# A short convolution in 8 steps of 16 channels, half-row matmuls in pairs, and a new written order, in a two-layer SSM and MLP kernel

## The chip, the cores and the metric

The kernel runs on one core of one Trainium2 chip. The metric is the device time of one execution in microseconds (us). The kernel before takes 224.44 us, the median of three runs (224.42 to 224.55). A profile of one execution gives the time of every instruction on every engine. PE is the matrix engine (TensorE), PEld its weight loads, DVE is VectorE, ACT is ScalarE, POOL is GpSimd, and SP issues most of the DMAs.

## The reference, cut to what matters

```python
B, S, D = 1, 2048, 640; ks = 4; F = 1728            # bf16 tensors
def _A_ref(q, k, v, shift_k, ssm_k, ssm_D):          # q is the layer-normed x
    k_shift[s, d] = sum over t in 0..3 of k[s - 3 + t, d] * shift_k[d, ks - 1 - t]
    kv = k_shift * v
    y = causal convolution of kv with ssm_k along s (by FFT of length 2 S)
    y = y + kv * ssm_D
    return q * y
def _B_ref(x, w1, b1, w2):
    h = x @ w1 + b1                                  # 640 -> 1728
    return (h * tanh(softplus(h))) @ w2              # Mish, 1728 -> 640
x = A_q
h = x + _A_ref(layernorm(x), A_k, A_v, A_shift_k, A_ssm_k, A_ssm_D)
out = h + _B_ref(layernorm(h), B_w1, B_b1, B_w2)
```

Only the convolution along the sequence, the skip term `kv * ssm_D` and the two matmuls of the MLP matter for what follows.

## The kernel before, in words

The 2048 positions are seen as 128 partitions by 16 (`NT`) positions each. The 640 channels are five blocks of 128, and these are grouped into three chunks: blocks 0 and 1, blocks 2 and 3, and block 4.

The first half of the kernel does the long convolution by transforms written as matmuls. Every matmul result lands in one of eight PSUM banks and has to be copied out (evicted) by ACT or DVE before the bank can be used again. The steps, with the names that the written order uses:

- `k1pe`/`k1ev` (L625): the filter `ssm_k`, loaded as `rn`, is transposed on PE, eight 128x128 transposes for each half of a block, and evicted.
- `dadd` (L620): the skip term. `ssm_D` is loaded as one row and added to the first row of the transposed filter, which is position 0 of the filter, by one small instruction for each block on POOL (four) and DVE (one).
- `s1kpe`/`s1kev` (L543, L544): first transform of the filter. Two matmuls with 64 weight columns each write the two halves of a bank, and run side by side in the array.
- `ktpe`/`ktev` (L571), `ktsh` (L585): the key `A_k` is transposed into `kt_s` and a copy shifted by one partition is made on POOL.
- `wsh` (L501), `coef` (L493), `cfpe` (L487): the weights of the short convolution. One matmul spreads `shift_k` over 128 partitions, four DVE copies lay it into `coef` with zeros around it, and four POOL multiplications by a mask make banded weights.
- `kspe` (L595, L596) and `kv` (L600): the short convolution. A step takes 4 positions by 32 channels as its 128 rows. Each step needs one matmul with 128 output columns for its own positions and one with 96 columns for the carry from the step before. DVE multiplies each result with the value and so makes `kv`.
- `s2kpe`/`s2kev` (L652): second transform of the filter with the table `G`. `sw` (L668, L669) are DMAs that exchange neighbouring partitions of the result, in two pieces for each chunk.
- `s1v`, `s2v` (L685): the same two transforms for `kv`. `p2` (L710) and `p1` (L706) are the products with the filter, elementwise in bf16. For chunk 0 there are four pieces of 128x2048, and each piece has one `p2` and one `p1`: six of these eight run on DVE, two on POOL.
- `i1pe`/`i1ev` (L743, L744): first inverse transform. It needs all products of its chunk.

The second half is the MLP. `i2p` (L803) and `y` are the second inverse transform for each of 16 tiles of 128 positions. `lnx`, `wb`, `h`, `bn`, `pow`, `hc` are the elementwise parts and the second layer norm. The normalised tile `hc` is transposed: tiles 0 to 3 on PE with an eviction (`trpe` L850, `trev`), tiles 4 to 15 by a transposing DMA (`trd`, L839). The tiles form five units of 256, 256, 512, 512 and 512 columns. `m1pe` (L898) multiplies a unit with `w1`, `hb` (L903) applies Mish, `m2pe` (L915) multiplies with `w2`, and `res` (L921) adds the residual. 1728 is 13 blocks of 128 rows and one of 64. The 64 rows go through `m1pex` (L878) for two units, or two halves of one unit, at once; their results stand in the lower and the upper 64 partitions of `hbx`. In the second matmul they are contracted over all 128 partitions by L916, the last of 14 matmuls of each result: the weights `w2[:, 13]` and `w2h` hold the 64 rows in one half and zeros (`w2z`, `w2hz`) in the other.

`fz` (L468) and `wm` (L464) are matmuls on zeros that fill waits of PE.

The order of all instructions is a list of words, `ORDER`, written out by hand or by a search outside of the kernel. Each word names a step and its engine (t PE, a ACT, v DVE, p POOL, d a DMA on SP's queue, s one on ACT's). `_schedule` walks over it, gives PSUM banks out and estimates start times, and the steps are emitted by these. Every engine does its own steps in this order, and SP its DMAs.

Of the kernel before, what the change touches and what calls it, by code (L numbers as in the profile page):

```python
# [17 lines left out]
D = 640  # L18
# [8 lines left out]
d_id:s d_sk:s wz:v d_dr:s cz:v d_go:d d_n2:d wm:t fz0:t d_n0:d k1pe2x:t warm:a k1ev2x:a d_n3:d k1pe2y:t d_n1:d cfpe:t d_n4:d k1pe0y:t k1ev0y:a  # L27
k1pe0x:t k1ev2y:v dadd2:v s1kpe2_0x:t k1ev0x:v kz:p coef:v s1kpe2_2x:t s1kpe2_1x:t s1kpe2_1y:t s1kev2_1x:v s1kev2_0x:v s1kev2_1y:v s1kpe2_3y:t
s1kev2_3y:a k1pe3x:t k1ev3x:a s1kev2_2x:a k1pe1x:t k1ev1x:v k1pe1y:t w2hz:p dadd0:p wsh0:p dadd1:p k1pe3y:t dadd3:p k1pe4y:t k1ev1y:v k1pe4x:t
k1ev3y:v k1ev4x:v dadd4:p s1kpe1_2y:t k1ev4y:a s1kpe1_3x:t s1kpe1_0x:t s1kev1_0x:v s1kpe1_0y:t s1kpe1_1x:t s1kev1_1x:v s1kpe0_1x:t s1kpe1_3y:t  # L30
s1kpe4_0y:t s1kev1_2y:a s1kpe2_2y:t s1kev1_3x:a d_k3:d d_k2:d d_x0:d s1kev0_1x:a s1kev1_0y:v s1kev1_3y:a s1kev2_2y:a s1kpe3_0x:t s1kpe0_2y:t
s1kev0_2y:a s1kpe0_1y:t s1kev3_0x:a s1kpe2_3x:t s1kev2_3x:a ktpe3y:t s1kpe0_2x:t s1kpe4_2x:t s1kev4_2x:a s1kev4_0y:v ln1_2:v s1kev0_1y:v ln1_1:v
s1kpe4_1x:t s1kpe0_0x:t s1kev4_1x:a s1kpe4_2y:t s1kpe1_2x:t s1kev0_0x:v s1kpe0_0y:t d_k1:d d_g4:d s1kev1_2x:a d_k0:d d_g5:d s1kpe3_2x:t ktpe0y:t
s1kev0_2x:a ktpe1y:t d_v1:d ktev0y:v ktpe4y:t ktev3y:v s1kpe4_0x:t ktev1y:v ktev4y:v s1kev4_2y:a s1kev0_0y:a s1kev3_2x:a s1kpe3_1y:t s1kev4_0x:a
s1kev3_1y:a s1kpe3_3x:t s1kpe3_0y:t s1kpe4_1y:t s1kev3_3x:a s1kpe0_3y:t s1kpe4_3y:t s1kpe2_0y:t s1kpe4_3x:t s1kev0_3y:v s1kev2_0y:v s1kev4_1y:a
ln1_3:v s1kev3_0y:a s1kev4_3x:a wsh1:p s1kpe3_2y:t ln1p1:p s1kpe3_1x:t s1kpe1_1y:t ktsh1:p wsh3:p s1kpe0_3x:t s1kpe3_3y:t s1kev3_1x:a ktpe2y:t
s1kev0_3x:a s1kev4_3y:a s1kev3_2y:v s1kev1_1y:v ktpe4x:t ktpe3x:t ktev3x:v ktpe1x:t s1kev3_3y:a ktev1x:v ln1_0:v ktpe0x:t s2kpe_14y:t d_g6:d d_g0:d
# [137 lines left out]
def _schedule(ops):  # L175
# [7 lines left out]
    for word in ORDER:  # L183
# [6 lines left out]
        for rt in o.allocs:  # L190
            t, rt.slot = rt.ring.free()
            est = max(est, t)
# [23 lines left out]
        for rt in o.allocs:  # L216
            rt.ring.take(rt.slot, rt)
# [9 lines left out]
def _dve1(n):  # L227
    return 0.06 + 0.001045 * n
# [740 lines left out]
```

## Time and profile before

| | |
|---|---|
| median of three runs | 224.44 us |
| profiled execution, its own time | 224.86 us |
| span in its trace | 223.1 us |
| busy PE / DVE / ACT / POOL | 214.7 / 146.2 / 134.4 / 65.7 us |
| matmuls | 2598 |

The span is what the trace covers; the 1.76 us between it and the execution's own time lie around it. "Busy" of PE counts a matmul from its start to its modelled end, and matmuls overlap, so the start times of neighbouring matmuls tell how fast PE really runs.

### The profile page before, as it was taken

How to read it: one execution, taken by the hardware profiler on the slowest of the kernel's cores; microseconds unless marked ns; L12 is line 12 of the kernel's file. 1: busy time of each engine (PE TensorE's matmuls, PEld its weight loads, DVE VectorE, ACT ScalarE, POOL GpSimd, SP SyncE). 2: the span in 40 equal slices, each digit the busy share in tenths (PEclk: the TensorE clock that was granted, in tenths of full speed). 3: DMA queues.
4: the chain of work that ended last, by engine and by line, in shares of the span. 5: the costliest groups of instructions: out<-in, count | busy, mean ns of one | idle time of the engine just before them, and what ended most of it. 6: DMA issues, size and time to landing. Idle time of an engine off the chain costs nothing.

```text
span 223.1 us, 6218 instructions
## 1 busy us (share of the span) xinstructions
PE 214.7 (96%) x2598; PEld 162.1 (73%) x2598; DVE 146.2 (66%) x317; ACT 134.4 (60%) x268; POOL 65.7 (29%) x106
## 2 busy tenths in 40 slices
PE   7998899999999999999999999999999999999994
PEld 2988899999877999988887644576645445675773
DVE  0699989999999998999788898974400000004023
ACT  2689989999999999888870446800053454330000
POOL 1271950005596007235767714320000000000000
PEclk9999999999999999999999999999999999999999
DMA  6999991075999999100001401043350000000024
GB/s 214 388 408 424 408 413 69 3 203 193 277 290 283 319 351 347 62 3 0 3 0 32 88 0 31 0 91 60 88 179 0 1 0 3 0 0 0 32 82 153
DMA packets 27342, 30.68 MB, mean 138 GB/s; under 512 B 9393, under 2 KB 23730, under 8 KB 26930
## 3 DMA queue, kind: packets, MB, share of 16 engines
q1 hardware_dynamic: 26880, 30.10, 41.1%
q8 instruction: 20, 0.33, 0.6%
q10 hardware_dynamic: 338, 0.18, 0.3%
q14 instruction: 8, 0.07, 0.1%
q0 software_dynamic: 96, 0.00, 0.0%
HBM read 20.45 MB, written 2.62 MB: 103 GB/s over the span
## 4 chain that ended last, share of the span: by engine, by line
PE 64%; DVE 13%; DMA 7%; ACT 7%; POOL 5%; issue 2%; SPq 0%; DVEq 0%; ACTq 0%; POOLq 0%
PE ps L915 21%; PE ps L898 19%; ACT uv L419 6%; DMA x<-in_A_q_dram 5%; PE ps L743 4%; PE ps L744 4%; PE ps L652 3%; PE ps L543 2%; PE ps L571 2%; DMA rn<-in_A_ssm_k_dram 2%; DVE st L776 2%; DVE st L822 2%; PE ps L595 2%; POOL r L782 2%; PE ps L916 2%
## 5 line engine op out<-in xcount | busy, mean ns | idle before, releaser
L915 PE MATMUL ps<-rn,uv 128*128 128x320 bf16 (+2 forms) x416 | 61.1, 299 | 0.2 <-DVE x L921 0.2
L903 ACT ACTIVATE uv<-ps,b1s 128x512 bf16<-128x512 f32 (+1 forms) x65 | 35.4, 610 | 39.1 <-PE ps L898 38.5
L898 PE MATMUL ps<-G 128*128 128x512 bf16 (+1 forms) x325 | 58.6, 337 | 0.0
L915 PEld LDWEIGHTS <-uv 128*128 128x128 bf16 x416 | 40.2, 98 | 17.5 <-issue 0.4
L419 ACT CAST uk<-ps 128x512 bf16<-128x512 f32 (+1 forms) x96 | 48.7, 702 | 2.6 <-PE ps L544 1.6
L898 PEld LDWEIGHTS <-G 128*128 128x128 bf16 x325 | 31.2, 98 | 23.9 <-issue 1.1
L921 DVE TENSOR_TENSOR xb<-ps,xb 128x320 bf16<-128x320 f32 (+2 forms) x12 | 5.7, 487 | 36.3 <-PE ps L916 35.8
L419 ACT CAST uv<-ps 128x512 bf16<-128x512 f32 (+2 forms) x57 | 28.7, 845 | 0.0
L921 DVE TENSOR_TENSOR xa<-ps,xa 128x320 bf16<-128x320 f32 x12 | 5.9, 488 | 21.6 <-PE ps L916 21.6
L827 POOL TENSOR_TENSOR r<-ve,mhalf 128x1 f32<-128x1 f32 x16 | 10.0, 630 | 32.7 <-DVE ve L824 32.7
L743 PE MATMUL ps<-a,uv 128*128 128x128 bf16 x160 | 18.8, 219 | 0.2
L421 DVE CAST uk<-ps 128x512 bf16<-128x512 f32 (+1 forms) x27 | 17.2, 669 | 1.4 <-PE ps L744 0.9
L743 PEld LDWEIGHTS <-uv 128*128 128x128 bf16 x160 | 17.9, 113 | 0.0
L421 DVE CAST uv<-ps 128x512 bf16<-128x512 f32 (+1 forms) x25 | 15.3, 677 | 0.0
L685 PE MATMUL ps<-uv,G 128*128 128x64 bf16 (+1 forms) x256 | 12.8, 197 | 0.8
L685 PEld LDWEIGHTS <-G 128*128 128x128 bf16 x256 | 11.1, 96 | 3.1 <-issue 2.1
L600 DVE TENSOR_TENSOR ra<-ps,rb 128x512 bf16<-128x512 f32 x20 | 12.5, 684 | 0.3 <-PE ps L596 0.3
L419 ACT CAST rb<-ps 128x512 bf16<-128x512 f32 (+1 forms) x28 | 10.6, 495 | 2.7 <-PE ps L803 2.7
L652 PE MATMUL ps<-uk,G 128*128 128x160 bf16 x128 | 12.1, 230 | 0.0
L782 POOL TENSOR_TENSOR r<-ve,mhalf 128x1 f32<-128x1 f32 x16 | 10.8, 672 | 1.3
L706 DVE TENSOR_TENSOR uv<-uv,uk 128x2048 bf16<-128x2048 bf16 (+1 forms) x11 | 10.9, 1022 | 0.0
L544 PE MATMUL ps<-cst,ra 128*64 128x128 bf16 x160 | 10.6, 220 | 0.1
(116 smaller groups left out, 376.7 us busy)
## 6 DMA issues: line engine op xcount, KB each, us to landing
G<-tab_g SPq DMA_DIRECT2D x8, 512.0 KB, 12.9
rn<-in_A_ssm_k_dram SPq DMA_DIRECT2D x5, 512.0 KB, 6.2
ra<-in_A_k_dram SPq DMA_DIRECT2D x4, 640.0 KB, 9.9
rb<-in_A_v_dram SPq DMA_DIRECT2D x2, 1280.0 KB, 13.1
G<-in_B_w_dram SPq DMA_DIRECT2D x5, 432.0 KB, 6.4
rn<-in_B_w_dram SPq DMA_DIRECT2D x1, 2080.0 KB, 9.8
rn<-uk SPq DMA_DIRECT2D x4, 512.0 KB, 5.1
rb<-uk SPq DMA_DIRECT2D x8, 256.0 KB, 7.9
```

The source lines that it names most:

```text
L419: nc.scalar.copy(o, i)
L421: nc.vector.tensor_copy(o, i)
L600: nc.vector.tensor_tensor(kv_w[:, m, :, 8 * h:8 * h + 8, l0:l0 + n], ps.rearrange("p (l t d) -> p d t l", l=n, t=8), raw_v[:, 8 * h:8 * h ...
L652: nc.tensor.matmul(ps[:, o:o + 160], g_v[:, f, :], KA[:, :, f, :], start=True, stop=True)
L685: nc.tensor.matmul(ps[:, fl * n:fl * n + n], g_v[:, f0 + h * kf + fl, :], VX[x][:, :, f0 + h * kf + fl, :], start=True, stop=True)
L706: eng.tensor_tensor(v, v, K[c.i][:, :, f0:f1, :], ALU.mult)
L743: nc.tensor.matmul(pz[:, k, :], V[c.i][:, dg // 4, :, dg % 4], a12[:, 0, :], start=True, stop=False)
L782: nc.gpsimd.tensor_tensor(r1[:, t2:t2 + 1], ve1[:, t2:t2 + 1], mhalf[:, 0:1], ALU.pow)
L898: nc.tensor.matmul(ph[:, 0:w], w1[:, dc, fc * P:fc * P + P], lnhT_of(u)[:, dc, 0:w], start=(dc == 0), stop=(dc == NDC - 1))
L903: nc.scalar.activation(hb_of(u)[:, fc, 0:w], rt.tile[:, 0:w], ACT.Mish, bias=b1s[:, fc:fc + 1], scale=1.0)
L915: nc.tensor.matmul(po[:, 0:d1 - d0], hb_of(u)[:, fc, tl * P:(tl + 1) * P], w2[:, fc, d0:d1], start=(fc == 0), stop=False)
L921: nc.vector.tensor_tensor(x, rt.tile[:, 0:d1 - d0], x, ALU.add)
```

## The change

The change has these parts.

- The short convolution takes 8 positions by 16 channels as its 128 rows. The carry needs 48 columns in place of 96. The counts stay: 80 matmuls of each kind, 20 multiplications on DVE. `kt_s` has three slots of eight groups (before five slots of four); `ktsh` copies twice as many elements. `wsh` is ten POOL multiplications of 128x704 in place of four of 128x1120, and stands in the free part of each `kt_s` block and in `xb`. `cfpe` lays the coefficients out with their zeros by nine matmuls, and `coef` is one copy of 128x440 on ACT.
- The skip term: `ssm_D` is loaded as 32 rows of 20, four small matmuls (`dcpe`) turn it into a column for each block, one DVE copy evicts it, and `dq` adds the column to the untransposed filter, one instruction of 128x1 on DVE for each block, before the half of the transposes that reads it.
- Tiles 2 and 3 (unit 1) are transposed by DMA: 14 transposing DMAs in place of 12, two `trpe` and two `trev` fewer.
- Row pairs: the 64 remaining rows are contracted first. `m2q` takes two tiles, one with its 64 rows in the lower partitions, one in the upper, and starts their results by matmuls that use 64 rows of the array each; it takes four PSUM banks. There are eight `m2q`. The zero halves and `w2z`, `w2hz` are gone. `m1pex` lays two units out so that the pair of a tile lies in the other half.
- The products of chunk 0 are eight pieces of 128x1024, eight of the sixteen on POOL and eight on DVE; the exchange of chunk 0 is four DMAs (`sw0_0` to `sw0_3`).
- Fillers: `wm` has eight matmuls in place of nine, each of the four `fz` has two in place of one, and no `fz` stands at the front.
- `ORDER` is new throughout, with other delays in the estimates (`d_k`, `d_n`, `sw0`, `d_t2m`, `d_w1`, the fetch of instructions). The filter begins with block 0 in place of block 2. The value's half `d_v1` is issued behind four of the eight pieces of `G`, before behind two. The table `t2m` is issued after the exchanges of chunks 1 and 2 and two pieces of `w1`, before between the exchanges of chunk 1 and chunk 2. On PE the words change between steps with the array in halves (`s1`, `m1pex`, `m2q`) and all others 54 times, before 28: 32 times up to the first `i1pe` (before 22) and 22 times after it (before 6).

```diff
@@ the skip term
-        def dadd(e, kd=kd, rd=rd):
-            k = kd[0:1, 0]
-            (nc.vector if e == "dve" else nc.gpsimd).tensor_tensor(k, k, rd, ALU.add)
+        def dadd(e, n=n, b=b):
+            nc.vector.tensor_tensor(n[:, 0:1], n[:, 0:1], d_col[:, b:b + 1], ALU.add)
+        k1 = OP(f"dq{b}", ("dve", 0.1), [d_n[b], d_rows], emit=dadd)
+    def emit_dc(e):
+        for a in range(4):
+            nc.tensor.matmul(ps_f32(dc_rt)[:, 0:NDC], cst[0:32, 4 * P + 3 - a:5 * P + 3 - a], d_row[:, a:20:4], start=(a == 0), stop=(a == 3))
@@ the weights of the short convolution
     def emit_cfpe(e):
-        nc.tensor.matmul(ps_f32(cf_rt)[:, 0:80], rep4, sk_r[:], start=True, stop=True)
+        ps = ps_f32(cf_rt)[:, 0:440]
+        for i, (a, j0, j1) in enumerate(((0, 0, 4), (4, 0, 4), (7, 1, 4), (7, 0, 1), (1, 0, 4), (2, 0, 4), (3, 0, 4), (5, 0, 4), (6, 0, 4))):
+            nc.tensor.matmul(ps.rearrange("p (r t) -> p r t", t=11)[:, :, a + j0:a + j1], cst[0:16, 3 * P - 16 * a:4 * P - 16 * a],
+                             sk_r[:].rearrange("p (r j) -> p r j", j=4)[:, :, j0:j1], start=(i == 0), stop=(i == 8))
     def emit_coef(e):
-        for a in range(4):
-            ps = slice(a * 32, a * 32 + 32)
-            nc.vector.tensor_copy(coef[ps, :, a:a + 4], cf_rt.tile[ps, 0:80].rearrange("p (g j) -> p g j", j=4))
+        ev(e, coef[:], cf_rt.tile[:, 0:440])
@@ the short convolution
-                for l in (2 * k, 2 * k + 1):
-                    r = 4 * m + l
-                    for a in (2 * h, 2 * h + 1):
-                        o = ps[:, (l - 2 * k) * 256 + (a - 2 * h) * P:][:, 0:P]
-                        nc.tensor.matmul(o, t[:, l, a, :], wsh[r // 5][:, r % 5, 0:128], start=True, stop=False)
-                        nc.tensor.matmul(o[:, 0:96], t[:, l, a - 1 if a else 4, :], wsh[r // 5][:, r % 5, 128:224], start=False, stop=True)
+                for l in range(4):
+                    o, q, w = ps[:, P * l:P * l + P], 4 * k + l, wsh[m][k][:, l, :]
+                    nc.tensor.matmul(o, t[:, q, h, :], w[:, 0:128], start=True, stop=False)
+                    nc.tensor.matmul(o[:, 0:48], t[:, q, 0 if h else 2, :], w[:, 128:176], start=False, stop=True)
@@ the products of chunk 0, the transposes
-        npf = (32, 32, 32)[len(c.dcs) - 1]
+        npf = (16, 32, 32)[c.i]
-        if U_OF[t2] >= 2:
+        if U_OF[t2] >= 1:
@@ the row pairs
+            def pq(e, ab=ab, parts=parts):
+                for i in range(2):
+                    for t2 in ab:
+                        _, c, h = last64[t2]
+                        d0, d1, rt = parts[t2][i]
+                        rhs = w2h[64:P, d0:d1] if h else w2[0:64, 13, d0:d1]
+                        nc.tensor.matmul(ps_f32(rt)[:, 0:d1 - d0], hbx[64 * h:64 * h + 64, c:c + P], rhs, start=True, stop=False)
                     for fc in range(NFC - 1):
-                        nc.tensor.matmul(po[:, 0:d1 - d0], hb_of(u)[:, fc, tl * P:(tl + 1) * P], w2[:, fc, d0:d1], start=(fc == 0), stop=False)
-                    nc.tensor.matmul(po[:, 0:d1 - d0], lhs, w2h[:, d0:d1] if h else w2[:, 13, d0:d1], start=False, stop=True)
+                        nc.tensor.matmul(po[:, 0:d1 - d0], hb_of(u)[:, fc, tl * P:(tl + 1) * P], w2[:, fc, d0:d1], start=False, stop=(fc == NFC - 2))
@@ the fillers
-        for _ in range(9):
+        for _ in range(8):
```

331 lines of the change are left out of this document (171 added, 160 removed).

## The prediction

> **What bounds the kernel now.** I read the page's busy shares and slices first, then the busy time by stage, then single stretches. From the page:
>
> ```profile
> span 223.1 us, 6218 instructions
> ...
> PE 214.7 (96%) x2598; PEld 162.1 (73%) x2598; DVE 146.2 (66%) x317; ACT 134.4 (60%) x268; POOL 65.7 (29%) x106
> ...
> PE   7998899999999999999999999999999999999994
> ...
> DVE  0699989999999998999788898974400000004023
> ACT  2689989999999999888870446800053454330000
> ```
>
> PE is busy nearly everywhere, but so are DVE and ACT in the first 40% of the slices. The view of busy time by stretches separates them (columns: length, then PE, PEld, DVE, ACT, POOL busy with instruction counts, clock, DMA share, GB/s):
>
> ```profile
> 5.70:28.00 22.30, 20.39 (x472) 19.32 (x473) 19.72 (x41) 19.05 (x33) 12.58 (x14) 1.00 1.02 407
> 28.00:72.00 44.00, 42.46 (x905) 39.33 (x904) 43.08 (x67) 43.19 (x93) 18.11 (x16) 1.00 0.69 215
> 72.00:124.00 52.00, 51.81 (x623) 45.83 (x621) 47.23 (x115) 40.68 (x94) 23.50 (x46) 1.00 0.38 124
> 124.00:220.00 96.00, 95.87 (x595) 56.30 (x594) 35.36 (x94) 30.00 (x49) 10.48 (x21) 1.00 0.16 41
> ```
>
> I read two regimes. From 28 to 72 us (conv, second transforms, products) both evicting engines are full, 43.1 and 43.2 of 44 us: this stretch lasts as long as DVE and ACT together have work, and a matmul removed there frees time on an engine that waits for banks anyway. From 5.7 to 28 us DMA is full (407 GB/s, share 1.02), and DVE and ACT have gaps of 2.6 and 3.25 us. From 72 us on PE is without gaps (0.2 and 0.1 us idle), so there each matmul taken away shortens the kernel by its pitch. The granted clock is 1.00 in all of it.
>
> **The late part, 72 to 220 us.** Three things change: the 64-row contraction, its mode switches, and two transposed tiles. The chain of work shows what one matmul costs in the stream, as pieces with start and length:
>
> ```profile
> 126.06 0.14 PE ps L916
> ...
> 168.88 14.03 PE ps L898 x65
> 182.91 1.20 PE ps L878 x10
> ```
>
> 65 matmuls of 512 columns take 14.03 us, 0.216 each. One L916 of 320 columns is 0.14 (0.135 by the same rate). There are 32 of L916: 30 of 320 columns, one of 512, one of 128, together 30 x 0.135 + 0.216 + 0.054 = 4.3 us. The change issues as many, but two at a time on separate halves of the rows. If two run in the time of one, 2.15 us go. The trace of before has no halves by rows; its nearest is L878, halves by columns: ten matmuls of 512 columns in 1.20 us, which is five times 0.216 and 0.12 over. So halves by columns do overlap fully. For halves by rows the ends are 0 and -2.15; I take -2.15, by L878. The Trainium skill (TensorE: Matmul & The Clock Gate, Part 3) states that matmuls on different row strips run concurrently, which no run here shows; by it the value is the same.
>
> What speaks against it is the change of mode. In the timeline around the same L878:
>
> ```profile
> 181.67 1.24 PE L898 MATMUL ps<-G 128*128 128x512 bf16 x5
> 182.84 1.27 PE L878 MATMUL ps<-G 128*64 128x512 bf16 x10
> 184.04 0.82 PE L898 MATMUL ps<-G 128*128 128x512 bf16 x3
> ```
>
> Five L898 fill 181.67 to 182.84 = 1.17 us, 0.09 more than 5 x 0.216; the halves fill 1.20, 0.12 more. A visit to half mode and back costs 0.21 us. Eight `m2q` stand alone among full matmuls (22 changes of mode after the first inverse transform, before 6), so 8 x 0.21 = +1.7 us. The ends are 0 (a change by rows is free) and +1.7; I take +1.7. The pairs bring only -2.15 + 1.7 = -0.45 us. By the skill's figure of some 4 ns for each further tile (the same section) the pairs would be worth the whole -2.15; the rows above give no reason to leave the switches out.
>
> `m2q` also takes four of eight banks at once and waits for `hbx`. Behind it on PE stand the `m2pe` of the same pair, so a late bank stops PE. The cover is that ACT is busy 30.0 of 96 us and DVE 35.4: results are evicted at once. Without it each `m2q` would cost an eviction of about 0.5 us.
>
> The tiles moved to the transposing DMA:
>
> ```profile
> 96.15 0.44 PE L850 MATMUL ps<-cst,hc 128*128 128x128 bf16 x5
> 96.43 0.60 PE L803 MATMUL ps<-uk,ra 128*128 128x256 bf16 x4
> ```
>
> ```profile
> L839 SPq DMA_TRANSPOSE G<-hc x12: 1199/1212/2358, 116.2 to 162.9; - x12
> ...
> DMA to landing us min/median/max: 2.6/2.6/3.7
> ```
>
> Five transposes fill 0.28 us, so two tiles give -0.56 us of PE, and two evictions leave ACT. In place of it come two issues of 1.2 us on SP and 2.6 us to the landing: `trd3` lands 1.2 + 2.6 = 3.8 us after `hc3`, or 5.0 if `trd2` is still to be issued. The new order puts seven `m1pe0` of 256 columns (5 x 0.108 each) and five `i2pc` (2 x 0.054) behind `hc3` before the first `m1pe1`, 4.3 us. I cost the landing at 0, with +0.7 as its other end. SP has nothing else then: w2 and x1 are issued before. Late sum: -0.45 - 0.56 = -1.0 us, with ends -2.7 (free switches) and +1.8 (no overlap, late landing).
>
> **The front, 5.7 to 72 us.** First the engines that bind, DVE and ACT (groups by line, with total and mean):
>
> ```profile
> L706 DVE TENSOR_TENSOR uv<-uv,uk 128x2048 bf16<-128x2048 bf16 x7 | 8.3, 1215 | 0.0
> ...
> L710 DVE TENSOR_TENSOR rb<-rb,uv 128x1024 bf16<-128x1024 bf16 x8 | 5.3, 683 | 0.0
> ...
> L706 POOL TENSOR_TENSOR uv<-uv,uk 128x2048 bf16<-128x2048 bf16 x1 | 4.1, 4083 | 0.0
> ...
> L493 DVE CAST coef<-ps 32x80 bf16<-32x80 f32 x4 | 1.0, 240 | 0.0
> ```
>
> ```profile
> L419 ACT CAST uk<-ps 128x480 bf16<-128x480 f32 x35 | 17.6, 682 | 0.8 <-ACT uv L419 0.8
> ...
> L824 DVE TENSOR_SCALAR ve<-mv 128x1 f32<-128x1 f32 x16 | 2.5, 153 | 0.6
> ...
> L620 DVE TENSOR_TENSOR rb<-rb,rn 1x128 bf16<-1x128 bf16 x1 | 0.2, 214 | 0.0
> ```
>
> ```profile
> 9.94 2.07 POOL L501 TENSOR_TENSOR xb<-cst,coef 128x1120 bf16<-128x1120 bf16 x1 [0.46 <-DVE coef L493]
> ```
>
> Chunk 0's products on DVE: six of 1.215 (7.3 us) become eight of 0.683 (5.5): -1.8. `coef`: -1.0 on DVE; on ACT one copy of 440 columns, by 17.6/35 for 480 columns +0.46. Skip term: -0.21, then six instructions of 128x1 (five `dq`, the copy before them), at 0.153 each +0.92. Sum -1.8 - 1.0 + 0.46 - 0.21 + 0.92 = -1.6 us of work, shared by two full engines -0.8 us. The other evictions keep number and size; the order only deals them anew. The ends are 0 (the work saved sits beside a gap) and -1.6 (all on the engine that ends last).
>
> POOL pays: `wsh` ten of 704 columns instead of four of 1120, by L501's 2.07 us about 13 us for 8.3; begun near 10 us and with the small steps between they are done near 25 us, before the convolution at 29.4; and eight products of 2.04 (half of 4.08), 16.3 us for 8.2. POOL is busy 18.1 of 44 us in the middle stretch, so it holds them; its cover fails only in the rival below.
>
> PE in the front. The start times of the short convolution:
>
> ```profile
> 29.43 0.22 PE L595 MATMUL ps<-hc,uv 128*128 128x128 bf16 x1
> 29.48 0.20 PE L596 MATMUL ps<-hc,uv 128*128 128x96 bf16 x1
> 29.52 0.22 PE L595 MATMUL ps<-hc,uv 128*128 128x128 bf16 x1
> ```
>
> A pair takes 0.09 to 0.10, of it 0.04 for 96 columns; 48 columns take between half of it and all, so 80 of them give 0 to -1.6 us. Against it stand eight more `cfpe` (32 x 40 = 1280 columns, 0.54), four `dcpe` (under 0.2), four more filler matmuls (4 x 0.216 = 0.86), and ten more changes of mode (1.0). PE's work in the front rises by 1 to 2.6 us, and I cost it at nothing, because PE waits for banks there: it has 905 matmuls in 44 us. If DVE and ACT stopped binding, it would come in full.
>
> What the order can win are gaps: 2.6 + 3.25 us in 5.7 to 28, 0.9 + 0.8 in 28 to 72, 7.5 us on two engines, so at most -3.8 us. I take a quarter, -0.9: `s1k` no longer waits for POOL's add, and block 0's eight groups come straight behind its transposes. What it can lose is bounded by the late value half:
>
> ```profile
> 10.84 0.33 SPq L520 DMA_DIRECT2D rb<-in_A_v_dram  x1
> ```
>
> ```profile
> rb<-in_A_v_dram SPq DMA_DIRECT2D x2, 1280.0 KB, 13.1
> ```
>
> ```profile
> 30.02 3.70 DVE L600 TENSOR_TENSOR ra<-ps,rb 128x512 bf16<-128x512 f32 x6 [0.33 <-PE ps L596]
> ```
>
> It was issued at 10.84 and landed about 13.1 later, at 24; two more pieces of `G` (1.05 MB) ahead of it cost 2.6 us at 407 GB/s, so 26.5; the first product with it ran at 30.02. The margin of 3.5 us covers it. The other half of the value and four pieces of `G` wait on SP behind the last `s1kpe2`, as before. `t2m` comes later behind the exchanges; its first reader, `i2pa0`, stands behind all inverse transforms. I cost both at 0; ends 0 and +1.5.
>
> **Sum.** Late -1.0, work -0.8, gaps -0.9: -2.7 us. The profiled execution took 224.86 us (span 223.1 and 1.76 around it), so 222.1; it stood 0.4 above the median of 224.44, against which I give the time: 221.7 us. About 0.2% (0.45 us) is what a measurement of this kernel can tell from no change.
>
> **Rivals.**
>
> *More is won.* The switches by rows are free (-1.7 more) or the order closes half of the gaps (-1.0 more): 218.8 to 220.7. For it speaks that ACT waits 3.25 us in 22.3; against it the 0.21 us a visit costs at L878. Chance 0.17.
>
> *Little is won.* Row halves do not overlap: late is -0.56 + 1.7 = +1.1 in place of -1.0, so 223.8; with the gaps kept too, 224.7. Nothing in the trace of before speaks for it but that it shows no row halves. Chance 0.13.
>
> *Slower: POOL and DVE block each other in chunk 0's products.* `i1pe` waits for all products of chunk 0, and eight are now on POOL, two of them (`p2_0_7`, `p2_0_4`) written between DVE's own. POOL's rows:
>
> ```profile
> 59.61 4.08 POOL L706 TENSOR_TENSOR uv<-uv,uk 128x2048 bf16<-128x2048 bf16 x1
> ...
> 63.78 1.08 POOL L781 TENSOR_SCALAR ve<-mv 128x1 f32<-128x1 f32 x1
> ...
> 66.45 1.78 POOL L783 TENSOR_SCALAR nmr<-mv,r 128x1 f32<-128x1 f32 x1
> ...
> 86.89 0.23 POOL L781 TENSOR_SCALAR ve<-mv 128x1 f32<-128x1 f32 x1
> ```
>
> ```profile
> 59.33 4.23 DVE L421 CAST uv<-ps 128x512 bf16<-128x512 f32 x7
> 63.48 2.42 DVE L710 TENSOR_TENSOR rn<-rn,uv 128x2048 bf16<-128x2048 bf16 x2
> ```
>
> While DVE multiplied in bf16 (from 63.48) POOL's L781 took 1.08 us in place of 0.23, 4.7 times; beside evictions from PSUM (59.33 to 63.56) its product took 4.08, undisturbed. If `p2_0_4` meets DVE's three products, 2.04 us become up to 9.6, +7.6. About ten halves of `s2vpe1` and a filler stand on PE between it and the first `i1pe`, some 3 us of cover: +4.6, so 226.3. It decides for slower once `p2_0_4` takes over 2.0 + 3 + 2.7 = 7.7 us. Against it: the written order puts four evictions from PSUM beside that product, as at 59.33. The Trainium skill (SBUF — State Buffer, section "SBUF: two separate sides") calls this an exclusive lock, held for a whole instruction, between GpSimd and a DVE instruction with two SBUF inputs; the trace agrees with 1.08 against 0.23. Chance 0.20, with which I also count a late landing.
>
> **How the numbers follow.** The forecast (220.7 to 223.5) has 0.50, more 0.17, little 0.13, slower 0.20. Of "little" I put 0.05 faster, 0.05 within 0.2%, 0.03 slower. Faster 0.50 + 0.17 + 0.05 = 0.72, same 0.05, slower 0.23. The range 218.6 to 225.6 takes in the second and third case and leaves out half of the slower one and the last bit of the better.
>
> **What will show it.** In the profile after: pitch of L916's successor, two matmuls of 320 columns within about 0.14 us; 0.2 us around each `m2q`; L850 with 10 in place of 20; six products of 1.2 us replaced by eight of 0.68 on DVE; POOL's products at about 2.0 us; no PE gap before `m1pe1`. The prediction is wrong if POOL's products take over 4 us, if PE waits for `t2m`, the key or the value, or if half mode by rows runs one matmul after the other.

## The result, and the profile after

The changed kernel takes 223.47 us (median of 20 executions), the kernel before 224.61 us beside it; the ratio is 0.9943 with a 95% interval of 0.9925 to 0.9961. That is 1.3 us won by the ratio (1.14 by the medians) where 2.7 were forecast. One thing is needed to read the numbers: 16 of the 20 executions took 222.2 to 224.3 us (the lower group) and four took 225.8 to 226.2 (the upper group), a ratio leaves out executions more than 1.5% above the fastest of their kernel, here these four, and the profile taken first is one of them. The profile read below is that of a further execution of the same kernel, at 222.92 us.

From its page:

```profile
span 221.1 us, 6309 instructions
...
PE 214.3 (97%) x2623; PEld 158.6 (72%) x2623; DVE 144.7 (65%) x323; ACT 134.4 (61%) x264; POOL 72.9 (33%) x112
```

Busy time by stretches, with the columns of the prediction:

```profile
5.70:28.00 22.30, 22.30 (x455) 20.19 (x454) 18.05 (x38) 19.56 (x34) 17.22 (x24) 1.00 1.02 411
28.00:72.00 44.00, 42.18 (x942) 38.26 (x942) 43.74 (x73) 43.50 (x94) 24.66 (x24) 1.00 0.70 194
72.00:124.00 52.00, 52.00 (x629) 45.66 (x627) 49.12 (x121) 41.46 (x92) 21.50 (x43) 1.00 0.52 154
124.00:220.00 96.00, 93.76 (x593) 52.97 (x591) 33.25 (x91) 28.38 (x45) 9.30 (x19) 1.00 0.16 43
```

From 5.7 to 28 us PE went from 20.39 to 22.30 of 22.3 us, and DVE from 19.72 down to 18.05. To see where the time was won, I cut both executions at the same instruction, the first matmul of the first inverse transform. Its row in the timeline of the kernel before, and of the changed one:

```profile
68.63 0.22 PE L743 MATMUL ps<-a,uv 128*128 128x128 bf16 x1
```

```profile
68.47 0.22 PE L751 MATMUL ps<-a,uv 128*128 128x128 bf16 x1
```

Behind it lie 223.1 - 68.63 = 154.5 us before and 221.1 - 68.47 = 152.6 us after. In the first profile, at 225.78 us, the cut is at 71.39 and 152.6 us follow as well. So the part behind the cut won 1.8 us in both profiles, and the front won 0.2 us here and lost 2.8 us there. The prediction had it the other way round: 1.0 late, 1.7 in front.

Not all of the 1.8 us is won by what the prediction had priced as late. The pairs and the moved transposes lie behind the second inverse transform, whose first matmul stands, before and after, at:

```profile
88.87 0.38 PE L803 MATMUL ps<-uk,ra 128*128 128x256 bf16 x2
```

```profile
88.27 0.38 PE L809 MATMUL ps<-uk,ra 128*128 128x256 bf16 x2
```

From the cut to there it takes 20.24 us before and 19.80 after, so 0.44 us are won in the first inverse transform by the new order, and 1.40 us behind it.

### The profile page after: what moved, and what is told of

Read it like the earlier page. It is cut to its first block, busy times and chain, and to the rows that moved or that the text cites. A ratio compares the mean times of both kernels' runs of the same rounds, so it can differ in the third digit from the quotient of the medians.

```text
span 224.0 us, 6309 instructions
## 1 busy us (share of the span) xinstructions
PE 216.7 (97%) x2623; PEld 160.8 (72%) x2623; DVE 146.1 (65%) x323; ACT 134.5 (60%) x264; POOL 72.9 (33%) x112
## 4 chain that ended last, share of the span: by engine, by line
PE 80%; ACT 12%; DMA 2%; DVE 2%; issue 2%
PE ps L939 25%; PE ps L906 25%; ACT uv L423 7%; ACT uk L423 5%; PE ps L751 4%; PE ps L809 4%; PE ps L558 4%; PE ps L658 4%; PE ps L752 4%; DMA rn<-in_A_ssm_k_dram 2%; PE ps L631 2%; PE ps L605 2%; PE ps L693 2%; PE ps L927 1%; PE ps L886 1%
## 5 line engine op out<-in xcount | busy, mean ns | idle before, releaser
L906 PE MATMUL ps<-G 128*128 128x512 bf16 (+1 forms) x325 | 58.9, 337 | 0.0
L939 PE MATMUL ps<-rn,uv 128*128 128x320 bf16 (+2 forms) x416 | 58.2, 299 | 0.0
L939 PEld LDWEIGHTS <-uv 128*128 128x128 bf16 x416 | 39.3, 98 | 17.9 <-issue 1.3
L423 ACT CAST uk<-ps 128x512 bf16<-128x512 f32 (+2 forms) x88 | 47.4, 716 | 5.0 <-PE ps L559 3.7
L906 PEld LDWEIGHTS <-G 128*128 128x128 bf16 x325 | 31.0, 98 | 24.4 <-issue 1.2
L423 ACT CAST uv<-ps 128x512 bf16<-128x512 f32 (+2 forms) x61 | 32.7, 773 | 0.1
L425 DVE CAST uk<-ps 128x512 bf16<-128x512 f32 (+1 forms) x35 | 21.8, 666 | 3.6 <-PE ps L559 3.1
L833 POOL TENSOR_TENSOR r<-ve,mhalf 128x1 f32<-128x1 f32 x16 | 10.0, 632 | 26.7 <-DVE ve L830 26.7
L751 PEld LDWEIGHTS <-uv 128*128 128x128 bf16 x160 | 17.9, 114 | 0.3 <-issue 0.2
L718 POOL TENSOR_TENSOR rn<-rn,uv 128x1024 bf16<-128x1024 bf16 x5 | 10.6, 2124 | 9.3 <-ACT uv L423 8.9
L425 DVE CAST uv<-ps 128x512 bf16<-128x512 f32 (+1 forms) x21 | 13.3, 677 | 0.1
L559 PE MATMUL ps<-cst,ra 128*64 128x128 bf16 x160 | 10.9, 221 | 0.0
L558 PE MATMUL ps<-cst,ra 128*64 128x128 bf16 x160 | 10.8, 220 | 0.0
L809 PE MATMUL ps<-uk,ra 128*128 128x256 bf16 (+1 forms) x96 | 10.6, 255 | 0.0
## 6 DMA issues: line engine op xcount, KB each, us to landing
G<-tab_g SPq DMA_DIRECT2D x8, 512.0 KB, 11.4
```

Source lines behind the costliest of these rows:

```text
L423: nc.scalar.copy(o, i)
L425: nc.vector.tensor_copy(o, i)
L558: nc.tensor.matmul(ps[0:64, k, :], lhs, mc, start=True, stop=True)
L751: nc.tensor.matmul(pz[:, k, :], V[c.i][:, dg // 4, :, dg % 4], a12[:, 0, :], start=True, stop=False)
L809: nc.tensor.matmul(py, t2m[:, t2, ri, :], Z[c.i][:, ri * NT + t2, :], start=(ri == 0), stop=(ri == 1))
L906: nc.tensor.matmul(ph[:, 0:w], w1[:, dc, fc * P:fc * P + P], lnhT_of(u)[:, dc, 0:w], start=(dc == 0), stop=(dc == NDC - 1))
```

## The experiments

All times are medians in us with their range; ratios are against the kernel before, run on the same chip. "The cut" is the first matmul of the first inverse transform.

**The same kernel again, and a longer warm-up.** First the clock. Theory A: the front's gain is lost where the full clock comes late. Rival B: the front is bound elsewhere.

> The changed kernel once more, unedited. Two theories of where the forecast gain of the front (1.7 us) went. Clock theory: in the profile shown, the full TensorE clock was granted only from about 13 us, against 5 us before, and the transposes of the key up to there took 1.93 us instead of 1.23 us; executions with a late grant are the upper group of the times (225.8 to 226.2 us), the others lie at 222.2 to 224.3 us. Then an execution of the lower group has the full clock by about 6 us, its first matmul of the first inverse stage starts some 2.5 us earlier than the 71.4 us of the profile shown, at 68.5 to 69 us, and the median stays at 223.5 us. Rival, front bound elsewhere: also with the early clock that matmul starts no earlier than the 68.6 us of before, so all of the 1.1 us won lies behind it. The two exclude each other only if the start falls to 67.5 us or below.

Measured: 223.12 (222.87 to 224.09), ratio 0.9939 (0.9918 to 0.9959), the cut at 68.47. The start of 67.5 us or less, at which A would have excluded B, was not reached. The pace of the matmuls shows the clock (the column of the granted clock says 1.00 in both, but the trace has no record of it before 12.96 us in the one and 7.13 us in the other). Timeline of the execution at 225.78 us, then of this one:

```profile
5.72 1.93 PE L631 MATMUL ps<-cst,rn 128*128 128x128 bf16 x16 [0.60 <-DMA rn<-in_A_ssm_k_dram]
7.58 1.54 PE L499 MATMUL ps<-sk_r,cst 16*128 16x160 bf16 x9
```

```profile
5.41 1.89 PE L631 MATMUL ps<-cst,rn 128*128 128x128 bf16 x16
7.23 0.89 PE L499 MATMUL ps<-sk_r,cst 16*128 16x160 bf16 x9
8.05 0.71 PE L631 MATMUL ps<-cst,rn 128*128 128x128 bf16 x8
```

Sixteen transposes take 1.9 us in both; then this execution goes on at a quicker pace (nine `cfpe` in 0.89 us, eight transposes in 0.71) and the other does not (1.54, and 1.07 for eight transposes), up to about 13 us. In the kernel before, the transposes have the quick pace from the start:

```profile
5.71 1.23 PE L625 MATMUL ps<-cst,rn 128*128 128x128 bf16 x16 [0.29 <-DMA rn<-in_A_ssm_k_dram]
```

That the slow pace is the clock, the profile of a later run (`b3` below, an execution of 225.47 us) shows in the column itself, the third number from the end. The stretches are laid where it changes; eight transposes that start in the second of them take 1.07 us:

```profile
4.04:7.45 3.41, 2.50 (x31) 2.00 (x29) 0.91 (x3) 1.01 (x1) 0.00 (x0) 1.00 1.00 324
7.45:10.86 3.41, 3.41 (x53) 3.02 (x52) 1.19 (x5) 1.51 (x3) 0.42 (x1) 0.50 1.03 420
```

So the late clock costs 2.9 us in the execution of the upper group (cut at 71.39 against 68.47), and B holds for the lower group: with the early clock the cut is where it was before (68.63).

```diff
-        for _ in range(8):      # wm of the changed kernel
+        for _ in range(10):
```

> The changed kernel with the warm-up back at its old length: 10 matmuls of 512 columns in a row at the start instead of 8 (before had 9 and one filler behind them). Clock theory: the upper group of times vanishes; no execution is above 224.8 us, the median is 223.2 to 223.4 us, since only one execution in five was in that group. Rival (the late grant has nothing to do with the length of the warm-up): the upper group stays at about one in five. If the two matmuls (0.86 us at the half clock) push back the first transposes of the key, the time rises by up to 0.9 us instead.

Measured: 223.60 (222.82 to 224.80), ratio 0.9953 (0.9935 to 0.9972). No execution of twelve is above 224.8, but the median is 0.1 to 0.5 above that of the changed kernel.

The reverse, in the kernel before:

```diff
-        for _ in range(9):      # and the first filler fz0 behind it
+        for _ in range(8):      # no fz0
```

> The kernel before with its warm-up shortened as the change does: 8 matmuls in a row instead of 9 and no filler behind them. Clock theory: the kernel before then has an upper group too, of some executions 2 to 4 us above the others, with the full clock granted only from 9 to 14 us in their profile. Rival: it stays in one group at 224.4 us, and the late grant comes from what else the change has in the first 6 us (the column matmuls and the gap behind them).

Measured: 224.53 (223.98 to 226.43), ratio 1.0008 (0.9985 to 1.0031). Nine executions lie at 224.0 to 224.9, three at 226.1 to 226.4. So the shorter warm-up makes an upper group with the front of before too (by the times; none of these three executions was profiled). It explains one execution in four or five, and not why the others gain nothing in the front.

**The late part.** One part at a time is undone.

```diff
-   nc.tensor.matmul(ps_f32(rt)[:, 0:d1 - d0], hbx[64 * h:64 * h + 64, c:c + P], rhs, start=True, stop=False)   # m2q
+   nc.tensor.matmul(po[:, 0:d1 - d0], hbx[:, c:c + P], w2h[:, d0:d1] if h else w2[:, 13, d0:d1], start=False, stop=True)   # 14th in m2pe
```

> The changed kernel with the last 64 features as before: no pairs by halves of rows, each of the 32 outputs of the second MLP matmul adds them by a 14th matmul of 128 rows, with the zero halves of the weights written as before (two memsets on GpSimd). All else stays, the written order too. The prediction gave the pairs 2.15 us for the overlap less 1.7 us for 8 changes of the array's mode, net 0.45 us: then this kernel is 0.45 us slower than the changed one, at 223.9 us. From the changed profile, where the pairs overlap and a visit costs 0.096 us on entry and 0.092 us on exit, 8 x 0.188 = 1.5 us: 0.65 us slower, 224.1 us. If the visits cost more than shown, since they also tie two outputs to one release, it is not slower.

Measured: 224.89 (224.07 to 227.49), ratio 1.0024 (0.9993 to 1.0054). Its profile has the cut at 72.20 and a span of 225.7, so 153.5 us follow, 0.87 more than with the pairs. The pairs are worth about twice the 0.45 that was forecast. One visit in the changed kernel's timeline:

```profile
139.00 2.33 PE L906 MATMUL ps<-G 128*128 128x512 bf16 x10
141.26 0.31 PE L927 MATMUL ps<-rn,hbx 64*128 64x320 bf16 x1
141.27 0.31 PE L927 MATMUL ps<-w2h,hbx 64*128 64x320 bf16 x1
141.41 0.30 PE L927 MATMUL ps<-rn,hbx 64*128 64x320 bf16 x1
141.41 0.30 PE L927 MATMUL ps<-w2h,hbx 64*128 64x320 bf16 x1
141.64 3.71 PE L939 MATMUL ps<-rn,uv 128*128 128x320 bf16 x26
```

Two matmuls on different rows start 0.01 us apart and the next two 0.15 later: halves by rows overlap in full. Ten L906 at 0.216 end at 141.16, so the visit lasts from there to 141.64, 0.48 us, of which 2 x 0.135 is work: 0.21 us for the two changes of mode, as priced. Four whole matmuls would take 0.54, so eight such visits explain 0.5 of the 0.87; the rest I have not located.

```diff
-        if U_OF[t2] >= 1:       # tiles 2, 3 by the transposing DMA
+        if U_OF[t2] >= 2:       # trpe2 trev2 trpe3 trev3 in place of trd2 trd3
```

> The changed kernel with tiles 2 and 3 of the normalised rows transposed on TensorE again (10 matmuls of 128 columns, and two evictions on ScalarE) instead of by DMA. The prediction gave this part 0.56 us of TensorE, and nothing for the landing. Theory: 0.5 to 0.65 us slower, 223.9 us, and the part from the first inverse stage to the end takes 153.2 instead of 152.6 us. Rival, the transposing DMAs only replace one wait by another: 223.3 us.

Measured: 224.29 (223.14 to 227.25), ratio 0.9981 (0.9962 to 1.0001). The cut is at 71.81 of 225.2, so 153.4 us follow: the two tiles are worth 0.76 where 0.56 were forecast, and their landing costs nothing. Together with the pairs that is 1.63 us (in both runs the stretch from the cut to the second inverse transform is as in the changed kernel, 19.8 us). The stretch behind that point won 1.40: either something else in it costs 0.2 us, or the two parts do not simply add.

**The halves of the change joined.** Two kernels take the front of before and the late part of the changed kernel, joined at two places of the written order.

```diff
-ORDER of the kernel before; its m1pex, m2pe, trpe2, trpe3
+ORDER of the kernel before up to the seam (b1: first i2pa, c2: first i1pe), behind it that of the changed kernel
+m1pex, m2q, m2pe, trd2, trd3 of the changed kernel
```

> The front of the kernel before (its short convolution, skip term, warm-up and written order up to the first inverse stage) with the late part of the changed kernel (tiles 2 and 3 by transposing DMA, row pairs, its written order from there on). It splits the result into the two halves of the change. Theory, the front was worth nothing: 223.0 to 223.4 us, as the changed kernel, with no upper group of times, and the first matmul of the first inverse stage at 68.6 us as before. If the changed front is worth what the prediction gave it (1.7 us), this kernel is at 224.6 less 1.0 = 223.6 us in the prediction's own sum, and at 223.1 + 1.7 = 224.8 us if all that was measured came from the front. If the changed front even costs time, it is below 222.9 us.

Measured: 226.77 (226.40 to 227.43), ratio 1.0085 (1.0059 to 1.0112). It tells nothing of the halves: the seam left evictions on DVE ahead of the second inverse transform. Waits of this kernel between 86 and 101 us:

```profile
ACT rb L420 <- PE ps L802: 4.1, 5, 2.1
PEld L802 <- DVE uk L422: 2.4, 1, 2.4
PE ps L802 <- DVE uk L422: 2.1, 1, 2.1
```

> As the hybrid before it (the front of the kernel before, the late part of the changed one), but joined at the first matmul of the first inverse stage (68 us) instead of 20 us later, so that the written order of the whole inverse stage and of the layer norm behind it is that of the changed kernel; the earlier seam had left evictions of VectorE ahead of the second inverse stage, and TensorE waited 4.5 us for them. From the profiles the part from that matmul to the end takes 152.6 us in the changed kernel and 154.4 us before. Theory, the whole gain is of the late part: 224.6 - 1.8 = 222.8 us, below both kernels, and no upper group of times. Rival, the late part's gain needs the changed front (exchange landings, evictions moved ahead): 223.5 us or more.

Measured: 224.13 (223.21 to 225.16), ratio 0.9990 (0.9967 to 1.0012), no upper group. The cut is at 69.10 and 153.4 us follow, 1.1 less than before and 0.8 more than in the changed kernel. The forecast of 222.8 us failed, and the time lies where the rival had it (223.5 or more). The second inverse transform begins 19.81 us behind the cut, as in the changed kernel, so the 0.8 us are lost behind that. Whether the late part needs the changed front for them, or words written for one front do not fit another, these two runs cannot tell. The split by the cut in the profiles does not rest on them.

**Which engine holds the front?** Load is taken from PE, added to PE, or added to DVE.

```diff
+   emit=None if i in (0, 2) else ...                       # b2: fz0, fz2 gone
-   nc.tensor.matmul(o[:, 0:48], ..., w[:, 128:176], ...)   # b3
+   nc.tensor.matmul(o[:, 0:96], ..., w[:, 80:176], ...)
+   if (m, h, k) in ((1, 1, 0), (0, 1, 1), (1, 0, 1), (4, 0, 1)):
+       nc.vector.memset(hc_t[:, 0:D], 0.0)                 # b4, ahead of a kv product
```

> The changed kernel without its first two pairs of filler matmuls (four matmuls of 512 columns that compute nothing, at 18 to 21 us); the two pairs at 60 and 65 us stay. In the profile of the fast execution TensorE is busy for all of 5.7 to 28 us. Theory, TensorE bounds the front: 4 x 0.215 = 0.86 us less work, so the first inverse stage starts 0.5 to 0.86 us earlier and the kernel is at 222.3 to 222.7 us. Rival, VectorE and ScalarE bound the front (43.7 and 43.5 of 44 us busy from 28 to 72): the time stays at 223.1 us, and TensorE waits 0.86 us more ahead of the first inverse stage.

Measured: 223.47 (222.90 to 226.03), ratio 0.9972 (0.9937 to 1.0007): nothing won by 0.86 us less of PE.

> The changed kernel with the second matmul of each convolution step 96 columns wide, as before, instead of 48 (80 matmuls, 29 to 50 us; it adds other taps, so the output is not the reference's). TensorE gets 80 x 0.020 = 1.6 us more work in that stretch. Theory, TensorE bounds the front: the kernel is slower by 1.0 to 1.6 us, at 224.1 to 224.7 us. Rival, VectorE and ScalarE bound that stretch: slower by 0 to 0.3 us.

Measured: 224.21 (223.46 to 225.47), ratio 0.9968 (0.9949 to 0.9988): 0.7 to 1.1 us above the changed kernel's two medians, 223.47 and 223.12.

> The changed kernel with four memsets of 128 x 640 added on VectorE between the products of the convolution (31 to 46 us; they write a buffer that nothing reads), 4 x 0.325 = 1.3 us more work of VectorE, none of TensorE. Theory, VectorE bounds that stretch: slower by 0.9 to 1.3 us, at 224.0 to 224.4 us. Rival, TensorE alone bounds it: 0 to 0.3 us slower. Both this and the wider second matmul costing their full work would mean that the engines hand each other the bound, and that taking work from one alone wins little.

Measured: 224.23 (223.20 to 226.77), ratio 0.9974 (0.9947 to 1.0001): as much. Adding 1.6 us to PE or 1.3 to DVE costs some 0.9; taking 0.86 from PE wins nothing. That is how it looks where several engines are full. The ratios alone do not settle it: the intervals of `b3` and `b4` overlap those of the changed kernel.

**The additions of the skip term.** In the longer warm-up's profile two of the five instructions of 128x1 are not short. DVE's timeline there, and POOL's:

```profile
9.80 1.65 DVE L625 TENSOR_TENSOR rn<-rn,d_col 128x1 bf16<-128x1 bf16 x3
11.36 0.68 DVE L425 CAST uk<-ps 128x512 bf16<-128x512 f32 x1
11.96 1.03 DVE L625 TENSOR_TENSOR rn<-rn,d_col 128x1 bf16<-128x1 bf16 x1
```

```profile
10.06 1.37 POOL L513 TENSOR_TENSOR uv<-cst,coef 128x704 bf16<-128x704 bf16 x1 [9.63 <-ACT coef L423]
11.37 0.11 POOL L525 MEMSET mhalf<- 128x16 f32 x1
11.41 0.29 POOL L527 MEMSET uv<- 128x8 bf16 x5
11.61 2.70 POOL L513 TENSOR_TENSOR xb<-cst,coef 128x704 bf16<-128x704 bf16 x2
```

The third addition comes after POOL's first product has begun at 10.06 and ends when that does, near 11.4; the next begins at 11.96 within POOL's second product and lasts until near 13.0. In the profile at 222.92 us POOL begins at 10.25, three additions slip through in 0.29 us, and one takes 0.75. The Trainium skill (SBUF — State Buffer, section "SBUF: two separate sides") states that a DVE instruction with two SBUF inputs and a GpSimd instruction that reads SBUF exclude each other for the whole instruction; the rows agree, with 1.37 us held. The prediction named this lock for the products of chunk 0, where it cost one DVE instruction 0.4 us (shown below, with the rivals), and not for the additions, where it cost more.

```diff
-   nc.vector.tensor_tensor(n[:, 0:1], n[:, 0:1], d_col[:, b:b + 1], ALU.add)
+   nc.scalar.activation(n[:, 0:1], n[:, 0:1], ACT.Identity, bias=d_col[:, b:b + 1], scale=1.0)   # c1: all five; d1: blocks 1 to 4; d_col in f32
+   nc.vector.tensor_scalar(n[:, 0:1], n[:, 0:1], d_col[:, b:b + 1], None, ALU.add)               # d2: all five; d_col in f32
```

> The changed kernel with the five additions of the skip term (128 x 1 each) on ScalarE instead of VectorE; their column is kept in f32, all else is as it was. In the profiles so far one such addition takes 0.155 us, but where GpSimd already writes the shifted coefficient matrices (1.37 us each) it lasts until that instruction ends: the group of three plus the next one takes 0.29 + 0.75 us in one execution and 1.65 + 1.03 us in three others, and behind it TensorE waits 1.0 us for VectorE's eviction. Theory, VectorE and GpSimd block each other here: the first inverse stage starts 0.5 to 1.5 us earlier and the fast times lie closer together; 222.2 to 222.9 us, against 223.3. Rival, that stretch is hidden (TensorE, or ScalarE with 5 x 0.2 us more work, bounds it): 223.2 to 224.2 us.

Measured: 227.01 (225.15 to 227.66), ratio 1.0090 (1.0057 to 1.0123), the cut at 72.64. The first addition now stood behind an eviction of 1.01 us on ACT, PE waited for it, and the quick pace came only at 13.6 us. PE's timeline:

```profile
5.73 1.07 PE L633 MATMUL ps<-cst,rn 128*128 128x128 bf16 x8 [0.17 <-DMA rn<-in_A_ssm_k_dram]
8.10 1.07 PE L633 MATMUL ps<-cst,rn 128*128 128x128 bf16 x8 [1.30 <-ACT rn L627]
```

Eight transposes take 1.07 us, against 0.71 at the quick pace above. The run could not tell the lock from the clock. With the longer warm-up on top of it:

> The additions of the skip term on ScalarE and the warm-up back at 10 matmuls together. Theory (blocking and late clock, both): no upper group of times, 222.2 to 222.8 us. If only the clock matters: 223.6 us as with the longer warm-up alone. If the two matmuls more cost their 0.86 us: 0.4 us above the one with the additions on ScalarE alone, apart from the upper group.

Measured: 226.37 (225.91 to 227.33), ratio 1.0084 (1.0053 to 1.0115). The wait of PE is still there, and ten matmuls do not make up for it: in its profile the granted clock is 1.00 from 4.67 to 8.08 us and 0.50 from there to 14.91.

> The changed kernel with four of the five additions of the skip term on ScalarE; the first, on which the first transposes wait, stays on VectorE. Theory, VectorE held up by GpSimd: VectorE no longer loses 1.0 to 2.4 us at 9.5 to 13 us, TensorE no longer waits 1.0 us there, and the first inverse stage starts at 67.5 to 68.5 us where the full clock comes by 7 us; lower group of times 222.0 to 222.8 us. Rival, the loss is taken up later by ScalarE and VectorE, full from 28 us on: 223.0 to 223.6 us. The upper group (late clock) stays, one execution in five.

Measured: 223.57 (223.01 to 226.45), ratio 0.9970 (0.9946 to 0.9995), the cut at 68.55.

> The changed kernel with the five additions still on VectorE, in the form that takes the column as a scalar per row (one tensor operand, the column in f32) instead of two tensors. If only instructions with two tensor operands wait for GpSimd, each takes 0.06 to 0.2 us whatever GpSimd does, and the time is as with four on ScalarE, 222.0 to 222.8 us. If every small write of VectorE waits for it, nothing changes: groups of 1.0 to 1.65 us, 223.3 us.

Measured: 223.04 (222.49 to 226.15), ratio 0.9944 (0.9916 to 0.9973), the cut at 68.54. With one tensor operand the additions no longer wait:

```profile
L625 DVE TENSOR_SCALAR rn<-rn,d_col 128x1 bf16<-128x1 bf16 x5 | 1.0, 213 | 0.6 <-DMA rn<-in_A_ssm_k_dram 0.5
```

The lock is real and now gone, and yet the ratio is that of the changed kernel. Its loss lay beside other work, or was too small for these runs (the median is 0.1 to 0.4 us below those of the changed kernel).

> Four additions on ScalarE and the warm-up back at 10 matmuls. Theory (both): no upper group, lower group as with the additions on ScalarE alone or up to 0.4 us above it, 222.2 to 223.0 us, which beats both kernels. Rival, the upper group stays since another wait of TensorE in the first 8 us decides over the clock.

Measured: 223.87 (222.88 to 225.22), ratio 0.9968 (0.9945 to 0.9992). Three executions at 225.2 remain. In the profile of one the reason is another: the granted clock falls to half just ahead of the cut (here at 70.76), behind a stretch in which PE was busy 1.58 of 3.43 us:

```profile
60.50:63.93 3.43, 1.58 (x33) 1.12 (x33) 3.43 (x7) 2.79 (x7) 1.20 (x1) 1.00 0.81 181
63.93:67.34 3.41, 3.41 (x48) 3.41 (x45) 1.57 (x4) 3.08 (x7) 2.16 (x2) 0.50 1.06 284
```

**PE's work in the first 28 us, step by step.** On top of the additions with one tensor operand:

```diff
+   emit=None if i in (0, 2) else ...     # e1, e2, e3: fz0, fz2 gone
+   for _ in range(10):                   # e2: wm
+   s1kpe2_2y before ktpe3y; s1kpe1_3y, s1kpe4_3x before ktpe3x; k1pe3y before s1kpe1_1x   # e3: ORDER
```

> The changed kernel with the additions of the skip term in the form with a scalar per row, and without the first two pairs of filler matmuls (18 to 21 us). Theory, TensorE bounds the first 28 us and what it does later moves everything behind: 0.86 us less of it, first inverse stage at 67.7 to 68.0 us, lower group 0.4 to 0.8 us below that of the kernel with the additions alone (222.8), 222.0 to 222.4 us. Rival, VectorE and ScalarE, full from 28 us on, hold the front: 222.7 to 222.9 us, first inverse stage at 68.5 us.

Measured: 223.11 (222.51 to 225.91), ratio 0.9952 (0.9926 to 0.9979), the cut at 68.25.

> As the one before, with the warm-up back at 10 matmuls. Late-clock theory: no upper group (225.8 us and above), 222.2 to 222.9 us in all executions, the two matmuls costing at most 0.4 us of what the fillers gave. Rival: single executions above 225 us remain, since TensorE still waits somewhere in the first 8 us or at 62 us.

Measured: 223.16 (222.86 to 223.49), ratio 0.9946 (0.9932 to 0.9961). Six executions, none in an upper group, the narrowest range of all; not measurably quicker than the changed kernel.

> As the first of these three, and four pieces of TensorE's written order moved so that half-array and whole-array matmuls change over six times less before 28 us (each change costs 0.095 to 0.125 us, 0.68 us in all). Theory, TensorE bounds the first 28 us: 0.3 to 0.7 us below the first of the three, 221.5 to 222.0 us. Rival, VectorE and ScalarE hold the front, or a moved piece waits for its input: no faster, 222.0 to 222.9 us.

Measured: 223.74 (223.26 to 226.98), ratio 0.9968 (0.9955 to 0.9980): slower, not quicker. In its profile ACT waits 0.7 us, between 5.7 and 30 us, for transposes of the key that now stand behind words of the filter, so this run says little of PE's load. By the other two, PE's work in the first 28 us is not what holds the front. The view by stretches says what is full there. The kernel before, the changed one, and the first of these three:

```profile
12.00:28.00 16.00, 14.10 (x362) 13.30 (x360) 15.22 (x31) 14.94 (x28) 10.07 (x13) 1.00 1.02 413
28.00:68.50 40.50, 39.22 (x855) 36.55 (x854) 39.73 (x62) 39.69 (x85) 15.91 (x14) 1.00 0.67 208
```

```profile
12.00:28.00 16.00, 16.00 (x340) 14.35 (x340) 14.80 (x30) 15.70 (x29) 15.47 (x17) 1.00 1.03 416
28.00:68.50 40.50, 39.06 (x891) 35.45 (x890) 40.24 (x68) 40.00 (x86) 24.66 (x24) 1.00 0.67 186
```

```profile
12.00:28.00 16.00, 15.20 (x337) 13.97 (x337) 14.54 (x30) 15.94 (x28) 15.47 (x18) 1.00 1.02 415
28.00:68.50 40.50, 39.01 (x888) 35.36 (x882) 40.24 (x68) 40.00 (x86) 24.15 (x23) 1.00 0.67 189
```

ACT (fourth of the busy numbers) is busy 15.70 and 15.94 of 16 us from 12 to 28, before 14.94, and all but 0.5 of the 40.5 us behind. Taking 0.8 us from PE turned PE's full 16.00 into 15.20 and left ACT full.

## Why the prediction was wrong, by its own steps

**Direction** right, **size** not: -1.3 us for -2.7. That the time still lies inside the range is partly luck: the late part won more than its forecast, and made up for some of a front that won next to nothing.

**Late, -1.0 forecast, -1.4 measured** behind the start of the second inverse transform (-1.8 behind the cut). The mechanism was right in each point: row halves overlap, 0.21 us a visit, 10 in place of 20 L850 (now L856), no wait of PE ahead of `m1pe1`. Mis-sized were the pairs (0.45 forecast, 0.87 by the run without them) and the transposes (0.56, measured 0.76).

**Front, "work -0.8": this step failed.** It took -1.6 us off DVE and ACT together and shared it by two. Busy time from 5.7 us to the cut, before and after (columns PE, PEld, DVE, ACT, POOL):

```profile
5.70:68.63 62.93, 59.74 (x1326) 56.00 (x1327) 59.58 (x102) 58.87 (x118) 28.62 (x27) 1.00 0.79 279
```

```profile
5.70:68.47 62.77, 61.33 (x1343) 55.60 (x1340) 58.26 (x105) 59.53 (x119) 41.88 (x47) 1.00 0.79 266
```

DVE fell by 1.32, but ACT rose by 0.66. Together that is -0.66 of the -1.6, and on ACT the sign is wrong. A part of it was mis-sized: the products of chunk 0 on DVE went from 7.3 to 5.9 us (5.5 forecast), and the six small instructions of the skip term took 1.5 us (0.92 forecast), two of them held by the lock. The rest is the sharing. The forecast's saving was nearly all on DVE (products, `coef`, skip term), its one addition on ACT the copy of `coef`, which took 0.53 us. "Shared by two full engines" holds only if the order hands ACT's evictions over to DVE, and it handed over none: up to the cut ACT starts 117 evictions in both kernels (seven of them long copies of 1024 columns before, eight after), and DVE 58 before and 59 after. So DVE's saving became waiting: its gaps grew by 1.16 us (3.35 to 4.51), the end "0 (the work saved sits beside a gap)" that the prediction had named. ACT lost 0.82 us of gaps (4.06 to 3.24) to 0.66 us more of work, and the difference is the 0.16 us by which the cut moved.

In 12 to 28 us DVE then idles 1.2 us beside a full ACT. That ACT's chain is what now sets the cut fits every run: in the twelve profiles of the changed front with the additions on DVE, ACT is busy 59.5 to 60.2 us from 5.7 us to the cut, wherever the cut lies between 68.25 and 72.32, so every delay is a gap on ACT. But it is argued from these rows, which say where the time went and not why: a kernel with evictions of that stretch moved from ACT to DVE was not tried. Nearest to it are `d1` and `d2`, on one chip, with four additions on ACT or on DVE: 223.57 against 223.04 us, but with overlapping intervals and the cut at 68.55 and 68.54, which settles nothing.

**Front, "gaps -0.9": nothing came.** On the two engines together the gaps did close between 28 and 72 us (0.92 + 0.81 before, 0.26 + 0.50 after) and in ACT's first stretch (3.25 to 2.74), but DVE's gap in 5.7 to 28 us grew from 2.58 to 4.25: 7.56 before, 7.75 after. The gaps that ACT did lose were filled by its added work.

**"PE's added work costs nothing."** For 5.7 to 28 us the cover was thinner than said (PE is full after the change), but taking fillers and mode changes out again won nothing. From 29 us on, 1.6 us more of PE cost 0.9.

**What was left out:** the shorter warm-up. It stood in the list of changes and had no price. It costs some 2.8 us in one execution of five, which is nothing in the median of a few executions and much in one profile.

**The rivals.** POOL's products of chunk 0 were not held:

```profile
L718 POOL TENSOR_TENSOR rn<-rn,uv 128x1024 bf16<-128x1024 bf16 x5 | 10.6, 2126 | 8.6 <-ACT uv L423 8.4 <-DMA rn<-uk 0.3
L714 POOL TENSOR_TENSOR uv<-uv,uk 128x1024 bf16<-128x1024 bf16 x3 | 6.4, 2129 | 0.2
```

2.13 us each, where 2.04 were forecast and over 4 would have decided for slower. The lock did show on the other side. Of DVE's three products of this form two take 0.68 us, and the third, which starts within a product of POOL that lasts until 66.6, takes 1.10:

```profile
66.06 1.10 DVE L718 TENSOR_TENSOR rn<-rn,uv 128x1024 bf16<-128x1024 bf16 x1
```

```profile
64.48 2.13 POOL L718 TENSOR_TENSOR rn<-rn,uv 128x1024 bf16<-128x1024 bf16 x1 [0.26 <-DMA rn<-uk]
```

"Little is won" came out by size, but not by its mechanism. In "More is won" the two gains, 1.7 and 1.0, lead from 221.7 to 219.0 us, not 218.8; nothing else hangs on it.

## What to carry to other kernels

Where two engines are both full, price a saving on the engine that has no gap at that place, not as half of a sum: work taken from one helps only as far as the written order passes the other's work over, and here it passed none. Cut both profiles at one common instruction before looking for causes, and at a second one where the priced work begins; here the part behind the cut took 152.5 to 152.7 us in every profile that has the changed front and the changed late part untouched, while whole executions spread over 2 us and more. A warm-up is part of the sum: count the executions on either side of its edge, not only the median.

## What the runs showed of the hardware that I had not expected

With eight matmuls of 512 columns as warm-up (they end at 4.8 us, and `dcpe` and the filter's landing leave a gap behind them) the quick pace begins, by the first record of the granted clock, at 5.1 to 7.1 us in the profiles of the lower group and at 13.0 to 13.8 us in those of the upper, `b3` apart: eight transposes take 0.71 us or 1.07. With a wait of 1.30 us between 6.8 and 8.1 us (`c1`) five of eight executions took 226.9 us or more, and in the one that was profiled the quick pace begins at 13.6 us.

The full clock can also be lost again. In four profiles the granted clock falls to 0.50 and comes back to 1.00: for 3.41 us from 7.45 (`b3`), 91.78 (`b1`) and 63.93 us (`d3`), and for 6.83 us from 8.08 (`c3`). Each time PE had waited in the stretch ahead: it was busy 2.50 of 3.41 us in `b3`, 1.73 of 3.78 in `b1`, 1.58 of 3.43 in `d3` and 1.92 of 3.41 in `c3`. The Trainium skill (TensorE: Matmul & The Clock Gate, Part 1) states that the gate watches a free-running window of about 3.4 us; the spells of 3.41 us, and of twice that, agree. That an execution's phase against such a window decides would fit the two groups, but no run here tests it.

A DVE addition of one column lasts 0.155 us alone and up to 1.4 us beside a GpSimd product, by the accident of 0.2 us in that product's start (10.06 or 10.25 us); with the second operand as a scalar per row it takes 0.21 to 0.22 us beside the same products.
